# Part of an fp32 matmul in float32r passes, and one subtraction on GpSimd: linear attention and two feed-forward layers

## The chip, the cores and the metric

The kernel runs on one core of one Trainium2 chip. The metric is the device time of one execution in microseconds (us): 1692.37 us is the median of three runs of the kernel before (1692.07 to 1695.33).

## The reference

The program computes a linear attention and two feed-forward layers behind it, in float32:

```python
kv  = np.einsum('bhsd,bhse->bhde', k, v)          # 8 batches, 8 heads, 576 tokens, 64 columns
out = np.einsum('bhsd,bhde->bhse', q, kv)
x   = out / np.sqrt(np.mean(out * out, -1, keepdims=True) + 1e-06) * g_norm   # 4608 tokens x 512
h   = x @ w_in                                     # layer 1: 512 -> 2048 -> 512
g   = (a0 + a1*h + a2*h**2 + a3*h**3) / (1 + |b0|*|h| + |b1|*h**2 + 1e-06)
x   = g @ w_out
h   = x @ moe2_w_in                                # layer 2: the same sizes
g   = np.where(h >= 1, h, np.where(h <= -1, 0, (h + 1)**2 / 4))
y   = g @ moe2_w_out
```

## The kernel before, in words

The 4608 tokens are cut into 9 blocks of 512 (`j` = 0 to 8; the text counts them as block 1 to block 9). A batch has 576 tokens, so a block of 512 mostly lies across two batches: its `q` columns fall into two pieces, 64 + 448, 128 + 384, 192 + 320, 256 + 256 and so on; only the first and the last block lie in one batch.

Phase 0 is the attention and layer 1, phase 1 is layer 2. In phase 0 the attention of block `j + 1` is done in pieces between the layer steps of block `j`. A layer step `f` (16 of them for each block) makes a hidden tile `h` of 128 x 512 with 12 matmuls (lines 441 to 443), its nonlinearity on ScalarE and VectorE (lines 450 to 478), and 12 matmuls into four accumulators (lines 493 to 495). The second half of a step comes `LAG` = 3 steps after the first half, so that there is time for the nonlinearity.

A product in float32 is had in one of two ways. A native fp32 matmul passes over its columns four times; the trace shows it as two MATMUL instructions. The other way splits each operand into a high part (float32r) and a low part (the value less the high part, also float32r), and adds three products: high by high, high by low, low by high. Both layers go the second way. The high part is made by ScalarE (line 184), the low part by a subtraction on VectorE (`subtract`, line 189). In phase 0 the hidden value's parts are `gh` (ScalarE) and `gl` (line 478, VectorE).

The attention of a block has four pairs of heads, `p` = 0 to 3 (function `attention`). For each: `q` is loaded into an `io` buffer, `out_mm` (line 380) multiplies it by the block-diagonal `kvbd` of its batch in native fp32, one matmul for each batch piece; ScalarE squares the result (`sq`), splits it into `sqh` and, on VectorE, `sql` (line 404, names `a<-a,a` fp32r in the trace), and TensorE sums over the head with a matrix of ones (`ms_mm`, lines 390 and 391; only the second of these reads `sql`). The rest scales the output and splits it into `xh` and `xl`. The scratch tiles `a1` to `a4` have one buffer each.

`k^T v` of all batches is made in block 1 and written to DRAM; `kv_fetch` brings it back into one of two `kvbd` buffers. The `raw` ring has four buffers of 4 KB in each partition: batches of k and v and then weights, as they come from DRAM, stand in it until they are decoded.

The order of the instructions is not written out by hand. Every operation is recorded with an engine, a cost and a key (`prog.op`), and `prog.order` plays them through a list scheduler: each engine takes the ready operation with the smallest key. Each engine then works through its own list strictly in order. GpSimd (POOL) has no operation in the kernel before. All DMAs go through SyncE's queue.

Of the kernel before, what the change touches and what calls it, by code (L numbers as in the profile page):

```python
# [121 lines left out]
def kernel(  # L122
# [60 lines left out]
    def activate(key, out, in_, func=AF.Copy, reads=(), cost=C_SB, **kw):  # L183
        op(ACT, cost, key, lambda: nc.scalar.activation(  # L184
            out=out(), in_=in_(), func=func, **{k: v() if callable(v) else v for k, v in kw.items()}
        ), [in_, *reads], [out])

    def subtract(key, out, x, hi):
        op(DVE, C_TT, key, lambda: nc.vector.tensor_tensor(  # L189
            out=out(), in0=x(), in1=hi().bitcast(F32), op=ALU.subtract  # L190
        ), [x, hi], [out])

# [44 lines left out]
    def load(key, t, src, cost=0.7, reads=(), rows=P):  # L237
        op(SP, cost, key, lambda: nc.sync.dma_start(out=t()[:rows], in_=src), reads, [t])
# [120 lines left out]
    def kv_fetch(bb, key):  # L359
# [6 lines left out]

        op(SP, 1.0, key, fetch, [kvs[bb]], [kvbd[bb % 2]])

    def attention(j, p, key, o_ring="o", m_ring="m", tags=("a1", "a2", "a3", "a4")):

        q = new("io", key - 2)
        load(key - 2, q, qT[p][:, j * T:(j + 1) * T])
        o = new(o_ring, key)

        def out_mm():
            t0 = 0
            while t0 < T:
                bb, r = divmod(j * T + t0, S)
                n = min(T - t0, S - r)
                nc.tensor.matmul(  # L380
                    out=o()[:, t0:t0 + n], lhsT=kvbd[bb % 2]()[:, p, :], rhs=q()[:, t0:t0 + n],
                    start=True, stop=True,
                )
                t0 += n

        def ms_mm():
            if native:
                nc.tensor.matmul(out=ms(), lhsT=ones().bitcast(F32), rhs=sq(), start=True, stop=True)
                return
            nc.tensor.matmul(out=ms(), lhsT=ones(), rhs=sqh(), start=True, stop=False)  # L390
            nc.tensor.matmul(out=ms(), lhsT=ones(), rhs=sql(), start=False, stop=True)

        batches = {j * T // S, (j * T + T - 1) // S}
        op(PE, 0.86, key, out_mm, [q, *(kvbd[bb % 2] for bb in batches)], [o])
        native = j < 2
        if native:
            sq, rs, og, e = (new(t, key) for t in tags)
            activate(key, sq, o, AF.Square, cost=C_PS)
        else:
            sq, sqh, sql = new(tags[0], key), new(tags[1], key, F32R), new(tags[2], key, F32R)  # L400
            og, rs, e = new(tags[0], key + 0.1), new(tags[2], key + 0.1), new(tags[3], key)
            activate(key, sq, o, AF.Square, cost=C_PS)
            activate(key, sqh, sq)
            subtract(key, sql, sq, sqh)
        activate(key, og, o, scale=ghalf, cost=C_PS + C_AP)
        ms = new(m_ring, key)
        op(PE, 0.86 if native else 0.43, key, ms_mm, [ones, sq] if native else [ones, sqh, sql], [ms])

        activate(key, rs, ms, AF.Abs_reciprocal_sqrt, cost=C_PS, bias=EPS)
        activate(key, e, rs, AF.Square)  # L410
        add_multiply(key, e, ms, EPS, e)
        add_multiply(key, e, e, -3.0, rs)
        multiply(key, e, og, e)
        xh, xl = new("xh", key, F32R), new("xl", key, F32R)
        activate(key, xh, e)
        subtract(key, xl, e, xh)
        xs[0, j, p] = (xh, xl)

# [14 lines left out]
    def ffn_step(ph, j, f, s):  # L433
        h = new("h", s)
        whi, wlo = wsb[ph, f, 0]
        for p in range(KT):
            xh, xl = xs[ph, j, p]

            def in_mm(p=p, xh=xh, xl=xl):
                c = slice(p * P, (p + 1) * P)  # L440
                nc.tensor.matmul(out=h(), lhsT=whi()[:, c], rhs=xh(), start=(p == 0), stop=False)  # L441
                nc.tensor.matmul(out=h(), lhsT=whi()[:, c], rhs=xl(), start=False, stop=False)  # L442
                nc.tensor.matmul(out=h(), lhsT=wlo()[:, c], rhs=xh(), start=False, stop=(p == KT - 1))  # L443

            op(PE, 0.68, s, in_mm, [whi, wlo, xh, xl], [h])
        k = s + 0.5
        native = ph == 0 and j == 0
        if ph == 0:

            ah, u, t, r = new("ah", k), new("u", k), new("t", k), new("r", k)  # L450
            activate(k, ah, h, AF.Abs, cost=C_PS)
            activate(k, u, ah, AF.Identity, scale=lambda: absb()[:, 1:2], bias=lambda: absb()[:, 0:1], cost=0.71)
            activate(k, t, h, AF.Identity, scale=lambda: na()[:, 3:4], bias=lambda: na()[:, 2:3], cost=0.665)
            multiply(k, u, u, ah)
            multiply(k, t, t, h)
            add_multiply(k, t, t, lambda: na()[:, 1:2], h)
            activate(k, r, u, AF.Abs_reciprocal_sqrt, bias=1.0 + EPS)
            activate(k, r, r, AF.Square)
            add_multiply(k, u, u, 1.0 + EPS, r)
            add_multiply(k, r, t, lambda: na()[:, 0:1], r)  # L460
            if native:
                gh = new("gh", k)
                add_multiply(k, gh, u, -2.0, r)
            else:
                add_multiply(k, u, u, -2.0, r)
                g = u
        else:

            cl, g = new("u", k), new("t", k)
            op(DVE, C_TT, k, lambda: nc.vector.tensor_scalar(  # L470
                out=cl(), in0=h(), scalar1=-1.0, scalar2=1.0, op0=ALU.max, op1=ALU.min
            ), [h], [cl])
            activate(k, cl, cl, AF.Square, scale=0.5, bias=0.5)
            op(DVE, C_TT, k, lambda: nc.vector.tensor_tensor(out=g(), in0=cl(), in1=h(), op=ALU.max), [cl, h], [g])  # L474
        if not native:
            gh, gl = new("gh", k, F32R), new("gl", k, F32R)
            activate(k, gh, g)
            subtract(k, gl, g, gh)

        k = s + LAG + 0.5  # L480
        if f == 0:
            acc[ph, j] = [new(f"acc{m}", k) for m in range(4)]
        wohi, wolo = (w32[f], None) if native else wsb[ph, f, 1]
        first, last = f == 0, f == NF - 1
        for m in range(4):
            o = acc[ph, j][m]

            def out_mm(m=m, o=o):
                c = slice(m * P, (m + 1) * P)
                if native:  # L490
                    nc.tensor.matmul(out=o(), lhsT=wohi().bitcast(F32)[:, c], rhs=gh(), start=first, stop=last)  # L491
                elif ph == 0:
                    nc.tensor.matmul(out=o(), lhsT=wohi()[:, c], rhs=gh(), start=first, stop=False)  # L493
                    nc.tensor.matmul(out=o(), lhsT=wolo()[:, c], rhs=gh(), start=False, stop=False)  # L494
                    nc.tensor.matmul(out=o(), lhsT=wohi()[:, c], rhs=gl(), start=False, stop=last)  # L495
                else:
                    nc.tensor.matmul(out=o(), lhsT=gh()[:, c], rhs=wohi(), start=first, stop=False)  # L497
                    nc.tensor.matmul(out=o(), lhsT=gh()[:, c], rhs=wolo(), start=False, stop=False)  # L498
                    nc.tensor.matmul(out=o(), lhsT=gl()[:, c], rhs=wohi(), start=False, stop=last)  # L499

            op(PE, 0.86 if native else 0.68, k, out_mm, [wohi, gh] if native else [wohi, wolo, gh, gl], [o])
            if last:
                t = new(("r", "r", "a1", "a2")[m] if ph else "io", k)
                activate(k, t, o, cost=C_PS)
                dst = x2d[j, m] if ph == 0 else out[j * T + m * P:j * T + (m + 1) * P, :]
                stored = prog.buf(None)
                op(SP, 0.7, k, lambda t=t, dst=dst: nc.sync.dma_start(out=dst, in_=t()), [t], [stored])
                if ph == 0:
                    x2s[j, m] = stored
# [20 lines left out]
        kv_batch(bb, 1.05 + 2.0 * (bb - 2), 0.45)  # L530
    for j in range(NB):
        s0 = j * NF
        if 2 <= j + 1 < B:
            kv_fetch(j + 1, s0 - 1)
        if j + 1 < NB:
            for p in range(KT):
                attention(j + 1, p, s0 + (0.9 + 3.6 * p if j == 0 else 2.5 + 3.8 * p))
        for f in range(NF):
            ffn_step(0, j, f, s0 + f)
            if j == 0:  # L540
                weight_low(0, f, 1, NF + f + 0.5, w32[f], wsb[0, f, 1][0])
# [57 lines left out]
```

## Time and profile before

| | us |
|---|---|
| median of three runs | 1692.37 |
| the profiled execution, whole | 1694.58 |
| its span, first to last instruction | 1692.8 |

The first page of the profile gives for each engine its busy time, the share of the span and the number of instructions. PE is TensorE's matmuls, PEld its weight loads (which lie beside matmuls), DVE is VectorE, ACT is ScalarE, POOL is GpSimd.

Three views follow below. The windows view gives for a stretch `A:B` (us from the start of the span) its length, then each engine's busy time with its instruction count in brackets, in the order PE, PEld, DVE, ACT, POOL, then the granted TensorE clock (1.00 is 2.4 GHz), the share of the DMA engines and GB/s. The lines view gives line, engine, operation, `out<-in` by the program's names, shapes, count, then busy us and mean ns of one, then idle us of the engine ahead of them and what ended most of it. The timeline gives start in us, duration in us, engine, line, operation and count; a bracket is the idle time just before it and its releaser. A matmul's modelled duration overlaps the next one, and so does a VectorE operation's by some 0.09 us: the pace is read from start to start. Rows with x2 or x4 are neighbours of one line merged into one row; the shape is that of the first.

### The profile page before, as it was taken

The numbers are of one execution on the slowest core, as the hardware profiler recorded it, in microseconds if no ns is written. First come the engines' busy times: TensorE is split into PE (matmuls) and PEld (weight loads), VectorE is DVE, ScalarE is ACT, GpSimd is POOL, SyncE is SP. The second block draws the span as 40 slices with busy tenths as digits, with TensorE's granted clock in tenths as the row PEclk, the third lists the DMA queues.
The fourth block names the chain that finished last, engine by engine and source line by source line (L and its number), as shares of the span: only waits on it lengthen the run. The fifth ranks groups of instructions, "written<-read, shape, count | busy, mean of one in ns | idle before, by whom it ended". The sixth has DMA issues, their size and how long they took to land.

```text
span 1692.8 us, 20528 instructions
## 1 busy us (share of the span) xinstructions
PE 1668.5 (99%) x7688; PEld 1343.0 (79%) x7688; DVE 1197.2 (71%) x1896; ACT 956.5 (57%) x1599; POOL 0.2 (0%) x4
## 2 busy tenths in 40 slices
PE   6999999999999999999999999999999999999999
PEld 4555788888888888888888888888888888888887
DVE  6999999989899998989999963434343434343333
ACT  6777878787877878787886542323232323232222
POOL 0000000000000000000000000000000000000000
PEclk9999999999999999999999999999999999999999
DMA  7667101010100101010214410101010101000000
GB/s 267 221 241 237 58 29 50 4 44 7 47 7 15 39 4 50 1 50 1 75 38 160 162 51 0 51 0 51 0 51 1 50 1 44 7 13 20 0 26 25
DMA packets 40531, 93.07 MB, mean 55 GB/s; under 512 B 7856, under 2 KB 8624, under 8 KB 40432
## 3 DMA queue, kind: packets, MB, share of 16 engines
q1 hardware_dynamic: 40432, 91.77, 16.1%
q8 instruction: 60, 0.98, 0.2%
q14 instruction: 39, 0.32, 0.1%
HBM read 72.09 MB, written 19.66 MB: 54 GB/s over the span
## 4 chain that ended last, share of the span: by engine, by line
PE 93%; DMA 3%; DVE 2%; ACT 1%; issue 0%; SPq 0%; DVEq 0%; ACTq 0%
PE h L441 15%; PE h L443 15%; PE h L442 15%; PE acc L499 8%; PE acc L497 8%; PE acc L498 8%; PE acc L493 7%; PE acc L495 7%; PE acc L494 7%; PE o L380 2%; PE acc L491 1%; DMA raw<-in_w_dram 1%; DMA raw<-in_kv_dram 1%; PE m L321 1%; ACT a L184 0%
## 5 line engine op out<-in xcount | busy, mean ns | idle before, releaser
L441 PE MATMUL h<-xh,wih 128*128 128x512 f32 x1152 | 459.2, 399 | 3.5 <-DVE t L198 2.6
L443 PE MATMUL h<-xh,wil 128*128 128x512 f32 x1152 | 449.3, 390 | 0.0
L442 PE MATMUL h<-xl,wih 128*128 128x512 f32 x1152 | 449.0, 390 | 0.0
L184 ACT ACTIVATE u<-u 128x512 f32<-128x512 f32 x144 | 90.9, 632 | 357.9 <-DVE u L470 357.9
L441 PEld LDWEIGHTS h<-xh,wih 128*128 128x128 f32 x1152 | 216.8, 188 | 54.5 <-DVE t L198 3.8
L442 PEld LDWEIGHTS h<-xl,wih 128*128 128x128 f32 x1152 | 216.7, 188 | 47.7 <-issue 3.3
L443 PEld LDWEIGHTS h<-xh,wil 128*128 128x128 f32 x1152 | 216.7, 188 | 46.2 <-DVE wil L290 0.5
L470 DVE TENSOR_SCALAR u<-h 128x512 f32<-128x512 f32 x144 | 99.6, 691 | 183.7 <-PE h L443 183.7
L497 PE MATMUL acc<-woh,gh 128*128 128x512 f32 x576 | 224.1, 389 | 0.0
L498 PE MATMUL acc<-wol,gh 128*128 128x512 f32 x576 | 224.1, 389 | 0.0
L499 PE MATMUL acc<-woh,gl 128*128 128x512 f32 x576 | 224.1, 389 | 0.0
L198 DVE SCALAR_TENSOR_TENSOR u<-u,r 128x512 f32<-128x512 f32 x272 | 188.2, 692 | 22.9 <-ACT r L184 19.9
L493 PE MATMUL acc<-gh,woh 128*128 128x512 f32 x512 | 202.3, 395 | 0.0
L495 PE MATMUL acc<-gl,woh 128*128 128x512 f32 x512 | 199.4, 389 | 0.0
L494 PE MATMUL acc<-gh,wol 128*128 128x512 f32 x512 | 199.2, 389 | 0.0
L189 DVE TENSOR_TENSOR gl<-t,gh 128x512 fp32r<-128x512 f32 x144 | 99.6, 692 | 130.7 <-ACT gh L184 130.7
L474 DVE TENSOR_TENSOR t<-u,h 128x512 f32<-128x512 f32 x144 | 99.0, 688 | 100.3 <-ACT u L184 100.3
L184 ACT ACTIVATE gh<-t 128x512 fp32r<-128x512 f32 x144 | 90.9, 631 | 132.3 <-PE acc L498 131.7
L498 PEld LDWEIGHTS acc<-wol,gh 128*128 128x128 f32 x576 | 108.2, 188 | 22.6
L499 PEld LDWEIGHTS acc<-woh,gl 128*128 128x128 f32 x576 | 108.1, 188 | 22.4
L497 PEld LDWEIGHTS acc<-woh,gh 128*128 128x128 f32 x576 | 108.0, 188 | 22.3
L184 ACT ACTIVATE r<-u 128x512 f32<-128x512 f32 x144 | 91.1, 633 | 46.7 <-DVE u L194 46.2
(90 smaller groups left out, 2123.4 us busy)
## 6 DMA issues: line engine op xcount, KB each, us to landing
raw<-in_w_dram SPq DMA_DIRECT2D x64, 512.0 KB, 3.9
raw<-in_kv_dram SPq DMA_DIRECT2D x28, 512.0 KB, 4.9
io<-in_qT_dram SPq DMA_DIRECT2D x36, 256.0 KB, 2.9
x2d<-io SPq DMA_DIRECT2D x36, 256.0 KB, 2.3
io<-x2d SPq DMA_DIRECT2D x36, 256.0 KB, 2.7
out_dram<-r SPq DMA_DIRECT2D x18, 256.0 KB, 2.0
out_dram<-a SPq DMA_DIRECT2D x18, 256.0 KB, 3.9
raw<-in_kv_dram SPq DMA_DIRECT2D x7, 256.0 KB, 3.6
```

Source lines behind the costliest of these rows:

```text
L184: op(ACT, cost, key, lambda: nc.scalar.activation(out=out(), in_=in_(), func=func, **{k: v() if callable(v) else v for k, v in kw.items()} ...
L189: op(DVE, C_TT, key, lambda: nc.vector.tensor_tensor(out=out(), in0=x(), in1=hi().bitcast(F32), op=ALU.subtract), [x, hi], [out])
L198: op(DVE, C_STT if callable(add) else C_TT, key, lambda: nc.vector.scalar_tensor_tensor(out=out(), in0=x(), scalar=add() if callable(add) ...
L441: nc.tensor.matmul(out=h(), lhsT=whi()[:, c], rhs=xh(), start=(p == 0), stop=False)
L442: nc.tensor.matmul(out=h(), lhsT=whi()[:, c], rhs=xl(), start=False, stop=False)
L443: nc.tensor.matmul(out=h(), lhsT=wlo()[:, c], rhs=xh(), start=False, stop=(p == KT - 1))
L493: nc.tensor.matmul(out=o(), lhsT=wohi()[:, c], rhs=gh(), start=first, stop=False)
L494: nc.tensor.matmul(out=o(), lhsT=wolo()[:, c], rhs=gh(), start=False, stop=False)
L495: nc.tensor.matmul(out=o(), lhsT=wohi()[:, c], rhs=gl(), start=False, stop=last)
L497: nc.tensor.matmul(out=o(), lhsT=gh()[:, c], rhs=wohi(), start=first, stop=False)
L498: nc.tensor.matmul(out=o(), lhsT=gh()[:, c], rhs=wolo(), start=False, stop=False)
L499: nc.tensor.matmul(out=o(), lhsT=gl()[:, c], rhs=wohi(), start=False, stop=last)
```

## The change

Three parts.

1. From block 3 on (`j >= 2`), a piece of `q` with at least 256 columns is multiplied by `k^T v` in three float32r matmuls where there was one native fp32 matmul. Pieces with fewer columns stay native, as do blocks 1 and 2. For this `q` is split: `qh` on ScalarE into the tile `a2`, `ql` on VectorE into the tile `a4`.
2. `kv_split` splits `kvbd` of batches 1 to 7 into a high and a low half; both stand in one buffer of the `raw` ring until the last block that uses the batch.
3. In blocks 2 to 8 (`1 <= j < NB - 1`) the subtraction for `gl` is done by GpSimd; in block 9 and in phase 1 it stays on VectorE.

The core of the diff:

```diff
-    def subtract(key, out, x, hi):
-        op(DVE, C_TT, key, lambda: nc.vector.tensor_tensor(
+    def subtract(key, out, x, hi, pool=False):
+        op(POOL if pool else DVE, 1.3 if pool else C_TT, key, lambda: (nc.gpsimd if pool else nc.vector).tensor_tensor(
             out=out(), in0=x(), in1=hi().bitcast(F32), op=ALU.subtract
...
+    def kv_split(bb, key):
+        hl = new("raw", key, F32R, (P, 2 * DM))
+        f32 = kvbd[bb % 2]
...
+        op(ACT, C_SB, key, lambda: nc.scalar.activation(out=hl()[:, :DM], in_=src(), func=AF.Copy), [f32], [hl])
+        op(DVE, C_TT, key, lambda: nc.vector.tensor_tensor(
+            out=hl()[:, DM:], in0=src(), in1=hl()[:, :DM].bitcast(F32), op=ALU.subtract
+        ), [f32], [hl])
+        kvr[bb] = hl
...
+        native = j < 2
+        if not native:
+            qh, ql = new(tags[1], key - 0.1, F32R), new(tags[3], key - 0.1, F32R)
+            activate(key - 0.1, qh, q)
+            subtract(key - 0.1, ql, q, qh)
...
+                if not native and n >= T // 2:
+                    w = [kvr[bb]()[:, i * DM + p * P:i * DM + (p + 1) * P] for i in range(2)]
+                    for i, (a, x) in enumerate(((w[0], qh), (w[0], ql), (w[1], qh))):
+                        nc.tensor.matmul(
+                            out=o()[:, t0:t0 + n], lhsT=a, rhs=x()[:, t0:t0 + n], start=(i == 0), stop=(i == 2),
+                        )
+                    t0 += n
+                    continue
...
-            subtract(k, gl, g, gh)
+
+            subtract(k, gl, g, gh, ph == 0 and 1 <= j < NB - 1)
...
+        if j == 1:
+            kv_split(1, s0 - 1)
         if 2 <= j + 1 < B:
             kv_fetch(j + 1, s0 - 1)
+            kv_split(j + 1, s0 - 0.5)
```

The three places in the engines' lists that the prediction speaks of follow. The first is TensorE's list in block 4, where the attention of block 5 (256 + 256 columns) puts its first product into accumulator `o`; `acc` and `h` are the layer's matmuls around it. Before:

```order
L493 MATMUL acc_583_2603<-gh_3277,woh_1597 128x512
L494 MATMUL acc_583_2603<-gh_3277,wol_2045 128x512
L495 MATMUL acc_583_2603<-gl_3288,woh_1597 128x512
L380 MATMUL o_3367<-io_2743,kvbd_75 128x256
L380 MATMUL o_3367<-io_2743,kvbd_74 128x256
L441 MATMUL h_3373<-xh_2656,wih_209 128x512
L442 MATMUL h_3373<-xl_2666,wih_209 128x512
```

And of the change, at the same place:

```order
L526 MATMUL acc_602_2620<-gh_3319,woh_1587 128x512
L527 MATMUL acc_602_2620<-gh_3319,wol_1911 128x512
L528 MATMUL acc_602_2620<-gl_3327,woh_1587 128x512
L405 MATMUL o_3409<-a_714_3238,raw_2374 128x256
L405 MATMUL o_3409<-a_715_3287,raw_2374 128x256
L405 MATMUL o_3409<-a_714_3238,raw_2374 128x256
L405 MATMUL o_3409<-a_714_3238,raw_3231 128x256
L405 MATMUL o_3409<-a_715_3287,raw_3231 128x256
L405 MATMUL o_3409<-a_714_3238,raw_3231 128x256
L473 MATMUL h_3419<-xh_2675,wih_209 128x512
```

The two native matmuls (each is two instructions in the trace) have become two groups of three, whose operands are the tiles `a2`, `a4` and two `raw` buffers; the place between the layer's matmuls is the same.

The second is VectorE's list at the same place: one layer step, with the subtraction for `sql` (`a<-a,a`) in it. Before:

```order
L198 SCALAR_TENSOR_TENSOR t_3345<-t_3345,na,h_3317 128x512
L194 TENSOR_TENSOR u_3364<-u_3364,ah_3343 128x512
L189 TENSOR_TENSOR gl_3377<-u_3307,gh_3370 128x512
L189 TENSOR_TENSOR a_697_3407<-a_695_3381,a_696_3399 128x512
L198 SCALAR_TENSOR_TENSOR u_3364<-u_3364,r_3387 128x512
L198 SCALAR_TENSOR_TENSOR r_3387<-t_3345,na,r_3387 128x512
```

And of the change:

```order
L198 SCALAR_TENSOR_TENSOR t_3387<-t_3387,na,h_3359 128x512
L194 TENSOR_TENSOR u_3406<-u_3406,ah_3385 128x512
L189 TENSOR_TENSOR a_719_3453<-a_717_3427,a_718_3445 128x512
L198 SCALAR_TENSOR_TENSOR u_3406<-u_3406,r_3433 128x512
L198 SCALAR_TENSOR_TENSOR r_3433<-t_3387,na,r_3433 128x512
L198 SCALAR_TENSOR_TENSOR u_3406<-u_3406,r_3433 128x512
```

The row for `gl` is gone from VectorE and stands on GpSimd's list, which holds nothing else in these blocks; the others keep their order.

The third is SyncE's list at the turn from block 1 to block 2: `raw<-in_w_dram` are layer 2's weights, `x2d` the output of layer 1, `io<-in_qT_dram` the `q` of the next attention.

```order
-L238 DMA raw_1518<-in_w_dram 128x512
-L238 DMA raw_1560<-in_w_dram 128x512
-L238 DMA raw_1571<-in_w_dram 128x512
-L238 DMA raw_1595<-in_w_dram 128x512
-L507 DMA x2d<-io_1667 128x512
-L507 DMA x2d<-io_1675 128x512
-L507 DMA x2d<-io_1695 128x512
-L507 DMA x2d<-io_1701 128x512
-L238 DMA io_1718<-in_qT_dram 128x512
-L238 DMA io_1739<-in_qT_dram 128x512
```

The first weights of layer 2 were loaded here, six pieces ahead of their use; now the `raw` buffers hold the split `k^T v`, and these loads stand in blocks 6 to 8 and at the start of block 9, one or two at a time.

## Rows read from the trace of the kernel before

**Rows 1.** First page: busy us, share of the span, instructions.

```profile
PE 1668.5 (99%) x7688; PEld 1343.0 (79%) x7688; DVE 1197.2 (71%) x1896; ACT 956.5 (57%) x1599; POOL 0.2 (0%) x4
```

**Rows 2.** Windows view: two of the blocks the change touches, then block 9.

```profile
363.86:456.36 92.50, 92.50 (x409) 76.61 (x408) 84.68 (x133) 73.98 (x125) 0.00 (x0) 1.00 0.08 25
456.36:548.87 92.51, 92.51 (x410) 76.39 (x408) 84.69 (x133) 74.00 (x125) 0.00 (x0) 1.00 0.08 25
...
826.00:920.00 94.00, 94.00 (x416) 77.86 (x415) 93.79 (x158) 72.72 (x123) 0.00 (x0) 1.00 0.28 93
```

**Rows 3.** Timeline of TensorE: a plain stretch, then native products of q.

```profile
268.63 0.39 PE L493 MATMUL acc<-gh,woh 128*128 128x512 f32 x1
...
270.67 0.39 PE L493 MATMUL acc<-gh,woh 128*128 128x512 f32 x1
...
363.63 0.39 PE L495 MATMUL acc<-gl,woh 128*128 128x512 f32 x1
363.86 1.02 PE L380 MATMUL o<-io,kvbd 128*128 128x256 f32 x4
...
364.95 0.40 PE L442 MATMUL h<-xl,wih 128*128 128x512 f32 x1
...
641.07 0.39 PE L495 MATMUL acc<-gl,woh 128*128 128x512 f32 x1
641.29 1.08 PE L380 MATMUL o<-io,kvbd 128*128 128x448 f32 x4
...
642.50 0.39 PE L442 MATMUL h<-xl,wih 128*128 128x512 f32 x1
...
734.00 0.39 PE L495 MATMUL acc<-gl,woh 128*128 128x512 f32 x1
734.23 1.02 PE L380 MATMUL o<-io,kvbd 128*128 128x512 f32 x2
...
735.32 0.40 PE L442 MATMUL h<-xl,wih 128*128 128x512 f32 x1
```

**Rows 4.** Lines view, whole span: weight loads of line 380.

```profile
L380 PEld LDWEIGHTS o<-io,kvbd 128*128 128x128 f32 x120 | 21.1, 189 | 7.1 <-issue 2.9
```

**Rows 5.** Lines view, 456.4 to 548.9 us: subtractions on VectorE.

```profile
L189 DVE TENSOR_TENSOR gl<-u,gh 128x512 fp32r<-128x512 f32 x16 | 11.0, 688 | 0.8 <-ACT gh L184 0.6
...
L189 DVE TENSOR_TENSOR a<-a,a 128x512 fp32r<-128x512 f32 x4 | 2.8, 688 | 2.0 <-ACT a L184 2.0
```

**Rows 6.** Timeline of VectorE, then of ScalarE: around one `gl`.

```profile
260.57 0.69 DVE L194 TENSOR_TENSOR u<-u,ah 128x512 f32<-128x512 f32 x1
261.18 0.74 DVE L198 SCALAR_TENSOR_TENSOR t<-t,na,h 128x512 f32<-128x512 f32 x1
261.83 0.69 DVE L189 TENSOR_TENSOR gl<-u,gh 128x512 fp32r<-128x512 f32 x1
262.63 0.69 DVE L198 SCALAR_TENSOR_TENSOR u<-u,r 128x512 f32<-128x512 f32 x1
...
260.75 0.63 ACT L184 ACTIVATE gh<-u 128x512 fp32r<-128x512 f32 x1 [0.83 <-DVE u L198]
261.29 0.63 ACT L184 ACTIVATE r<-u 128x512 f32<-128x512 f32 x1
261.96 0.64 ACT L184 ACTIVATE r<-r 128x512 f32<-128x512 f32 x1
...
264.54 0.81 ACT L184 ACTIVATE u<-ah,absb 128x512 f32<-128x512 f32 x1
```

**Rows 7.** Timeline: `sql` on VectorE and the matmul that reads it, twice.

```profile
367.56 0.69 DVE L189 TENSOR_TENSOR a<-a,a 128x512 fp32r<-128x512 f32 x1 [1.96 <-ACT a L184]
...
369.07 0.39 PE L391 MATMUL m<-a,ones 128*128 128x512 f32 x1
...
387.73 0.69 DVE L189 TENSOR_TENSOR a<-a,a 128x512 fp32r<-128x512 f32 x1
...
388.80 0.39 PE L391 MATMUL m<-a,ones 128*128 128x512 f32 x1
```

More of the change, by code (lines that the diff above doesn't have):

```diff
@@ L367, in kv_fetch, with src @@
         op(SP, 1.0, key, fetch, [kvs[bb]], [kvbd[bb % 2]])
+    kvr = {}
+    def kv_split(bb, key):
+        hl = new("raw", key, F32R, (P, 2 * DM))
+        f32 = kvbd[bb % 2]
+        def src():
+            return f32().rearrange("p n d -> p (n d)")
+        op(ACT, C_SB, key, lambda: nc.scalar.activation(out=hl()[:, :DM], in_=src(), func=AF.Copy), [f32], [hl])
[3 more added lines that the diff above has]
+        kvr[bb] = hl
     def attention(j, p, key, o_ring="o", m_ring="m", tags=("a1", "a2", "a3", "a4")):
@@ L393, in attention @@
         batches = {j * T // S, (j * T + T - 1) // S}
-        op(PE, 0.86, key, out_mm, [q, *(kvbd[bb % 2] for bb in batches)], [o])
-        native = j < 2
+        if native:
+            op(PE, 0.86, key, out_mm, [q, *(kvbd[bb % 2] for bb in batches)], [o])
+        else:
+            op(PE, 0.73, key, out_mm, [q, qh, ql, *(t for bb in batches for t in (kvbd[bb % 2], kvr[bb]))], [o])
         if native:
```

## The prediction

> **What bounds the kernel now.** I read the first page for the engine that is busy throughout, then the windows view block by block, then TensorE's timeline at the places that change, and last VectorE and ScalarE around one `gl`. The page shows TensorE busy for 99% of the span and VectorE for 71% [rows 1]; the average hides that VectorE has nearly all its work in phase 0. The windows show it: from one attention product to the next block's, 92.5 us, TensorE is busy for the whole length, the clock is 1.00 (2.4 GHz), and VectorE is busy for 84.7 us, 92% [rows 2]. So in these seven blocks TensorE waits for nothing, and its own work is the bound. A matmul taken away there is worth its pace, and nothing else can make these blocks shorter. VectorE has 7.8 us of idle time in a block to take new work. The two things to price are therefore what TensorE saves, and whether VectorE and GpSimd still deliver in time.
>
> **What TensorE saves.** A plain float32r matmul of 512 columns goes every 0.2267 us (nine from 268.63 to 270.67) [rows 3]. At the granted 2.4 GHz 512 columns are 0.2133 us, so 0.0133 us belongs to the instruction. The native product of q of 512 columns costs this: from the last matmul ahead of it (734.00) to the second behind it (735.32) are 1.32 us, of which 0.453 are two plain paces, so 0.867 us [rows 3], four passes of 0.2133 and one 0.0133. With 256 + 256 columns it is again 0.867 (363.63 to 364.95), with 64 + 448 it is 0.977 (641.07 to 642.50). For pieces of N columns I set three passes of N / 2400 + 0.0133 us, and for a narrow piece that stays native four passes of N / 2400 (and 0.007, half of the 0.0133). For one pair of heads that makes
>
> - block 3 (128 native, 384 wide): 0.220 + 0.520 = 0.74, saves 0.127; block 7 has the same pieces
> - block 4 (192, 320): 0.327 + 0.440 = 0.767, saves 0.10; block 6 the same
> - block 5 (256 + 256, both wide): 6 x 0.120 = 0.72, saves 0.147
> - block 8 (64, 448): 0.217 (from the 0.977 less 0.76 for 448 columns) + 0.60 = 0.817, saves 0.16
> - block 9 (512): 0.68, saves 0.187
>
> Together 0.948 us, times four pairs of heads 3.8 us. That is all that can be had. The bounds: if the 0.0133 us fell away with short passes, 96 x 0.0133 = 1.3 us more (5.1); if a pass could not be shorter than the 0.189 us which a weight load takes [rows 4], 384, 320 and 256 columns would each cost three times 0.189 and only 0.7 us would be left. The row of block 8 speaks against the second: the two instructions for 64 columns, each with its own weight load, cost 0.217 us in all, 0.108 each [rows 3], so loads follow each other faster than their 0.189. I take 3.8.
>
> **What is added, and what hides it.** ScalarE gets one `qh` for each of 28 attentions and seven copies in `kv_split`: five instructions of 0.63 us in a block (the duration of `gh` [rows 6]), 3.2 us beside 74.0 of 92.5 [rows 2]. It stays below 85% and costs nothing. VectorE gets four `ql` and one low half of `k^T v` in a block and loses 16 `gl`, all the same kind of operation of 0.69 us [rows 5], which follow each other at 0.6 (260.57 to 261.18 [rows 6]): 84.7 - 9.6 + 3.0 = 78.1 us, so its idle time grows from 7.8 to 13.8 us in a block of about 92, 0.86 in each of 16 steps. That is the cover for `ql`. In TensorE's list the product that reads `ql` stands about a layer step behind it, so that wait is covered as well.
>
> The w2 loads that moved late cost nothing either: the decoded weights need slots which are free only once block 9 has used the first layer's, and there VectorE is already busy for 93.8 of 94.0 us [rows 2] without TensorE standing. The change moves no `gl` there.
>
> **The subtraction on GpSimd.** The trace has no such operation: POOL is busy for 0.2 us in all [rows 1]. The nearest row is the same subtraction on VectorE, 0.69 us, as the lower end. From above, what counts is how long it may take. In one step `gh` ends at 261.38, and ScalarE writes the next but one `u`, into the buffer that `gl` reads, at 264.54 [rows 6]: 3.1 us in which the subtraction is free for the ring. I take twice VectorE's row, 1.4 us. GpSimd then works a quarter of each step.
>
> The other question is what VectorE does meanwhile. Behind `gh` ScalarE makes the two `r` operations, and VectorE's `u<-u,r` needs the second: it ends at 262.60 and `u<-u,r` starts at 262.63, 1.25 us behind the end of `gh` [rows 6]. VectorE filled just this gap with `t<-t,na,h` (one operand in PSUM) and with `gl` itself. So GpSimd's `gl` falls into a time in which VectorE, without `gl`, has to wait for ScalarE anyway; of 1.4 us 0.15 reaches beyond the gap, against 0.86 of idle time in a step. The Trainium skill (SBUF — State Buffer, Who interferes with whom) says that a VectorE instruction with two SBUF inputs and a GpSimd instruction which reads SBUF exclude each other, the second waiting for the whole of the first. By that rule alone every such pair that meets would be serial; in the gap there is none to meet, and no row here shows GpSimd at work. Its page GPSIMD Engine Reference (section 3.1, Elementwise) gives 4497 ns for 2048 elements, from which I estimate some 1.1 us for 512; with it the subtraction would just fit the gap, and the sum would be the same.
>
> Where the cover is thin is `sql`. The matmul that reads it starts 0.82 us behind the end of `sql` in one attention and 0.38 in the next [rows 7], and there are 28. A delay of VectorE beyond that stops TensorE's whole list. If a GpSimd subtraction stood ahead of all of them for its 1.4 us, they would wait 0.6 and 1.0, 28 x 0.8 = 22 us; with none it is 0. As GpSimd runs a quarter of the time and mostly in ScalarE's gap, I take 0.2 us in all, near the lower end.
>
> **The sum.** -3.8 + 0.2 = -3.6 us, in the profiled execution from 1694.6 (span 1692.8 and 1.8 around it) to 1691.0. That execution was 2.2 us above the median; the saving holds for both, so the median goes from 1692.4 to 1688.8.
>
> **Rivals.**
>
> - *TensorE waits at `sql`.* If VectorE comes later than the list assumes, by the odd GpSimd operation or by `ql` in front, the saving is eaten bit by bit: 0.12 us at each of 28 places is 3.4 us, 1692.1. For it: the 0.38 us, and a saving so small that little is needed. Against it: the idle time of VectorE nearly doubles.
> - *VectorE becomes the bound.* The place is `u<-u,r` behind GpSimd's subtraction: if that holds VectorE for more than its 0.86 us of idle time in each of 112 steps, every step grows by the rest. At 1.0 us this is 112 x 0.14 = 16 us, 1704; it decides (slower by more than 3.4 us) from 0.92 us. For it: operations with two SBUF inputs are more than half of VectorE's, and the attention's stand in no fixed place to `gh`. Against it: the 1.25 us gap. This is the time by the skill's rule if the two engines mostly meet.
> - *Short passes bound by weight loads*, worked out above: 0.7 us saved, 1691.7. The 64-column row is against it.
>
> **How the numbers follow.** What a measurement of this kernel can tell from no change is about 0.2%, 3.4 us, so faster means below 1689.0: the forecast lies just beyond it. I give the forecast 0.45 (0.40 of it below 1689.0), the waits at `sql` 0.27 (0.25 of it within 3.4 us, the rest slower), the weight loads 0.06, VectorE as the bound 0.22. So faster 0.40, same 0.05 + 0.25 + 0.06 = 0.36, slower 0.24. The likeliest case alone spans 1687.3 (the 5.1 us) to 1689.5. The range goes up into the two rivals, to 1699: 10 us of waits for `sql` or the beginning of the VectorE bound.
>
> **What would show it.** Right: the seven stretches in which the attentions of blocks 3 to 9 are done each shorter by 0.4 to 0.75 us in the windows view, TensorE busy throughout; `gl` on POOL of 1 to 1.5 us, ended before `u<-u,r` starts; VectorE at about 85% in these blocks, its operations at 0.69 us. Wrong: waits of TensorE for the `sql` subtraction or for `ql` that add up to microseconds; VectorE's two-input operations longer than 0.69 us beside POOL, or blocks that grow together with VectorE's busy time; three float32r passes of 256 columns above 0.36 us. A `gl` of over 3 us would make ScalarE's `u` wait for POOL.

## The result, and the profile after

The changed kernel takes 1715.46 us (median of four runs, 1714.10 to 1717.54) beside 1692.54 for the kernel before (now four runs): a ratio of 1.0137, 95% interval 1.0125 to 1.0149. It is slower by 23 us where 3.6 us less were forecast. The profiled execution took 1714.46 us with a span of 1712.7, 19.9 us more than the span before.

The windows view of the changed kernel, for the stretch that answers to the second of [rows 2] and for the next; the columns are the same:

```profile
463.51:558.49 94.98, 93.44 (x414) 76.41 (x413) 84.49 (x123) 74.93 (x129) 23.55 (x16) 1.00 0.11 35
558.49:654.80 96.31, 93.53 (x414) 76.35 (x412) 85.77 (x125) 76.22 (x131) 23.60 (x16) 1.00 0.11 35
```

The stretch is 2.5 to 3.8 us longer than the 92.5 us of before, and TensorE is no longer busy throughout. VectorE's busy time has not fallen: 84.5 us, where 78.1 were worked out, although 16 subtractions have left it. GpSimd's list is busy for 23.6 us.

Who TensorE waited for between 170 and 860 us, in the waits view (us in total, times, longest):

```profile
PE m L421 <- DVE a L189: 10.7, 20, 2.0
PE m L420 <- ACT a L184: 4.6, 9, 1.2
```

Both are the sum over the head (lines 390 and 391 of before): L420 reads `sqh`, L421 reads `sql`. Nothing else stops TensorE there. The view counts idle time against modelled ends, so it shows too little. So the waits are counted from start to start: from the matmul ahead of a sum to the one behind its two matmuls there should be three plain paces of 0.2267 us. What is beyond that adds up to 24.5 us over the 28 sums; in the kernel before it is 0.0. All waits at the sums that follow are counted in this way.

The saving on TensorE came as worked out. The product of q of 512 columns, the answer to the last three of [rows 3]:

```profile
751.09 0.39 PE L528 MATMUL acc<-gl,woh 128*128 128x512 f32 x1
751.32 0.84 PE L405 MATMUL o<-a,raw 128*128 128x512 f32 x3
...
752.23 0.39 PE L474 MATMUL h<-xl,wih 128*128 128x512 f32 x1
```

From 751.09 to 752.23 are 1.14 us, less two paces 0.687; the forecast was 0.68, and 0.867 before. The other pieces cost 0.757 (128 + 384), 0.767 (192 + 320), 0.72 (256 + 256) and 0.837 (64 + 448), each within 0.02 us of the forecast. Over all 28 products this comes to 3.7 us less than before. So -3.7 on the products and +24.5 at the sums make 20.8, near the 19.9 us of the span.

The lines view of VectorE between 175 and 845 us, and of GpSimd's `gl`, shows what became of the operations beside GpSimd:

```profile
L198 DVE SCALAR_TENSOR_TENSOR t<-t,na,h 128x512 f32<-128x512 f32 x112 | 82.8, 740 | 0.5
L194 DVE TENSOR_TENSOR t<-t,h 128x512 f32<-128x512 f32 x112 | 76.1, 680 | 3.8 <-ACT t L184 3.5
...
L194 DVE TENSOR_TENSOR u<-u,ah 128x512 f32<-128x512 f32 x112 | 89.6, 800 | 1.1 <-ACT u L184 0.7
L198 DVE SCALAR_TENSOR_TENSOR a<-a,a 128x512 f32<-128x512 f32 x28 | 26.2, 937 | 0.0
L189 DVE TENSOR_TENSOR a<-io,a 128x512 fp32r<-128x512 f32 x27 | 24.8, 917 | 0.2
...
L189 POOL TENSOR_TENSOR gl<-u,gh 128x512 fp32r<-128x512 f32 x112 | 157.4, 1405 | 680.9 <-ACT gh L184 622.2 <-PE h L475 27.8 <-DVE t L198 27.5
```

The two operations with one input in PSUM (`t<-t,h` and `t<-t,na,h`) kept their 0.68 and 0.74 us. Those with two inputs in SBUF are longer: `u<-u,ah` 0.80, `a<-a,a` 0.94 and `ql` (`a<-io,a`) 0.92 us, against 0.69. These means hide two kinds. A held `u<-u,ah` and a held `ql` are in the timeline of VectorE, then of GpSimd, at two places of block 5:

```profile
464.32 0.75 DVE L198 SCALAR_TENSOR_TENSOR t<-t,na,h 128x512 f32<-128x512 f32 x1
464.98 1.78 DVE L194 TENSOR_TENSOR u<-u,ah 128x512 f32<-128x512 f32 x1
...
479.74 1.52 DVE L189 TENSOR_TENSOR a<-io,a 128x512 fp32r<-128x512 f32 x1
...
464.92 1.29 POOL L189 TENSOR_TENSOR gl<-u,gh 128x512 fp32r<-128x512 f32 x1 [3.65 <-ACT gh L184]
...
479.42 1.29 POOL L189 TENSOR_TENSOR gl<-u,gh 128x512 fp32r<-128x512 f32 x1 [5.08 <-ACT gh L184]
```

At 464.92 GpSimd starts its subtraction, which ends at 466.21; `u<-u,ah` starts 0.06 us behind it and ends at 466.76, that is 0.55 us behind GpSimd's end: it stood still until GpSimd was done. This text calls that a hold. `ql` at 479.74 ends 0.55 us behind GpSimd's end (480.71) too. In this trace 62 VectorE operations are longer than 0.8 us, in all by 47 us more than 0.69 each. All 62 started while a GpSimd subtraction ran, and all read two operands in SBUF; 29 operations with an input in PSUM started there too, and none took more than 0.75 us. The other way round holds as well: 35 of GpSimd's 112 subtractions start while VectorE runs an operation with two SBUF inputs and take 1.65 us on average, the other 77 take 1.29. This is the rule of the Trainium skill (SBUF — State Buffer, Who interferes with whom), and the trace agrees: the second waits for the whole of the first.

How the hold reaches TensorE is in the timeline behind the first of these, of ScalarE, then of VectorE and TensorE:

```profile
465.14 0.62 ACT L184 ACTIVATE a<-o 128x512 f32<-128x512 f32 x1
466.80 0.63 ACT L184 ACTIVATE r<-u 128x512 f32<-128x512 f32 x1 [1.03 <-DVE u L194]
467.33 0.58 ACT L184 ACTIVATE io<-acc 128x512 f32<-128x512 f32 x1
467.81 0.62 ACT L184 ACTIVATE a<-a 128x512 fp32r<-128x512 f32 x1
...
468.46 0.69 DVE L189 TENSOR_TENSOR a<-a,a 128x512 fp32r<-128x512 f32 x1 [1.70 <-ACT a L184]
...
468.13 0.39 PE L528 MATMUL acc<-gl,woh 128*128 128x512 f32 x1
468.49 0.50 PE L420 MATMUL m<-a,ones 128*128 128x512 f32 x1
469.21 0.50 PE L421 MATMUL m<-a,ones 128*128 128x512 f32 x1 [0.22 <-DVE a L189]
```

`r` waits 1.03 us for the held `u<-u,ah`; `sqh` (`a<-a` fp32r at 467.81) has its input since 465.76, but stands two places behind `r` in ScalarE's list. `sql` starts at 468.46, behind it. TensorE, which runs its own list in order, reaches the sum before either is done: from start to start its last three matmuls here are 0.36 and 0.72 us apart, where the pace is 0.23.

### The profile page after: what moved, and what is told of

Its sections match the earlier page's. It is cut to its first block, busy times and chain, and to the rows that moved or that the text cites. A ratio compares the mean times of both kernels' runs of the same rounds, so it can differ in the third digit from the quotient of the medians.

```text
span 1712.7 us, 20776 instructions
## 1 busy us (share of the span) xinstructions
PE 1674.6 (98%) x7720; PEld 1344.8 (79%) x7720; DVE 1196.6 (70%) x1819; ACT 968.1 (57%) x1634; POOL 157.6 (9%) x116
## 4 chain that ended last, share of the span: by engine, by line
PE 65%; DVE 20%; ACT 8%; issue 3%; DMA 3%; POOL 0%; SPq 0%; ACTq 0%; DVEq 0%; POOLq 0%
PE h L473 11%; PE h L475 10%; PE h L474 10%; PE acc L532 8%; PE acc L531 8%; PE acc L530 8%; DVE u L198 5%; ACT r L184 3%; PE acc L526 3%; PE acc L527 3%; PE acc L528 3%; DVE r L198 3%; DVE u L194 2%; DVE t L194 2%; DVE a L198 2%
## 5 line engine op out<-in xcount | busy, mean ns | idle before, releaser
L198 DVE SCALAR_TENSOR_TENSOR u<-u,r 128x512 f32<-128x512 f32 x272 | 198.6, 730 | 53.1 <-ACT r L184 51.7
L189 POOL TENSOR_TENSOR gl<-u,gh 128x512 fp32r<-128x512 f32 x112 | 157.4, 1405 | 680.9 <-ACT gh L184 622.2
L184 ACT ACTIVATE gh<-u 128x512 fp32r<-128x512 f32 x128 | 81.0, 633 | 87.0 <-DVE u L198 82.7
```

Source lines behind the costliest of these rows:

```text
L184: op(ACT, cost, key, lambda: nc.scalar.activation(out=out(), in_=in_(), func=func, **{k: v() if callable(v) else v for k, v in kw.items()} ...
L189: op(POOL if pool else DVE, 1.3 if pool else C_TT, key, lambda: (nc.gpsimd if pool else nc.vector).tensor_tensor(out=out(), in0=x(), in1=h ...
L198: op(DVE, C_STT if callable(add) else C_TT, key, lambda: nc.vector.scalar_tensor_tensor(out=out(), in0=x(), scalar=add() if callable(add) ...
```

## The experiments

Two theories stand against each other first. Theory L: GpSimd's hold on VectorE (the lock, in the expectations) makes the sums late. Theory O: the new lists and the added ql, qh and splits do, whoever does `gl`. All ratios are to the kernel before, run on the same chip.

**gl back on VectorE**

```diff
-            subtract(k, gl, g, gh, ph == 0 and 1 <= j < NB - 1)
+            subtract(k, gl, g, gh)
```

> The changed kernel with all gl subtractions left on VectorE; the wide float32r pieces, ql, qh and the split of k^T v stay, and the lists are planned anew. Theory L (the lock): GpSimd's subtraction reads SBUF and holds VectorE's operations with two SBUF inputs, sql comes late, and TensorE waits at the 28 sums over the head; without it the waits at L421 fall from 15.8 us to under 2 and the time is 1688.5 to 1690.5. Theory O (order and load): the added ql, qh and splits leave too little ahead of the sums, whoever does gl; VectorE then has about 3 us more per block than in the kernel before, the waits stay or grow, and the time is above 1705.

Measured: 1688.80 us, ratio 0.9978 (0.9969 to 0.9988); the waits at the sums are 0.1 us. The windows view of this kernel between 175 and 845 us:

```profile
175.00:845.00 670.00, 670.00 (x2995) 556.42 (x2994) 640.54 (x1019) 556.89 (x946) 0.00 (x0) 1.00 0.10 33
```

TensorE is busy throughout, and VectorE is busy for 640.5 of 670 us, 96%, without making it wait. Theory O falls: the added work alone costs nothing. The whole of the 3.7 us is there (0.22% of 1692), and this version is faster than the kernel before by that little, and than the changed kernel by 1.6%.

**The kernel before with gl on GpSimd and nothing else**

```diff
-            subtract(k, gl, g, gh)
+            subtract(k, gl, g, gh, ph == 0 and 1 <= j < NB - 1)
```

in the kernel before, with the changed `subtract`.

> The kernel before with the gl subtraction of blocks 2 to 8 on GpSimd and nothing else changed (native products of q, no splits). Theory L: the same waits at the sums (L391) as in the changed kernel, some 20 to 26 us, and no saving: 1710 to 1719. Theory O: VectorE loses 9.6 us of work in a block and gets none, so nothing waits: 1690 to 1694.

Measured: 1695.85 us, ratio 1.0025 (1.0016 to 1.0034), slower by some 4 us, with 2.5 us of waits, nearly all at the first three sums. Both theories missed their ranges. The hold is there: 34 VectorE operations are longer than 0.8 us, in all by 18 us more than 0.69 each. Yet the waits are a tenth of those in the changed kernel. The lines view of its VectorE, 175 to 845 us, shows where the holds fall:

```profile
L194 DVE TENSOR_TENSOR u<-u,ah 128x512 f32<-128x512 f32 x115 | 78.7, 684 | 1.2 <-ACT u L184 1.2
L189 DVE TENSOR_TENSOR xl<-a,xh 128x512 fp32r<-128x512 f32 x28 | 26.2, 936 | 0.0
```

`u<-u,ah` is not held at all here (0.684 us); `xl` is (0.936), but no sum waits for `xl`. The same place of the timeline as above, in this kernel (VectorE, then GpSimd):

```profile
457.11 0.69 DVE L194 TENSOR_TENSOR u<-u,ah 128x512 f32<-128x512 f32 x1 [0.20 <-ACT u L184]
...
457.73 1.29 POOL L189 TENSOR_TENSOR gl<-u,gh 128x512 fp32r<-128x512 f32 x1 [4.48 <-PE o L380]
```

VectorE starts `u<-u,ah` 0.62 us ahead of GpSimd and is through 0.07 us behind GpSimd's start. In both lists `t<-t,h` and `t<-t,na,h` stand just ahead of it, in this order, and yet in the changed kernel it comes 0.06 us behind GpSimd. The next run shows why.

**The same lists, but GpSimd reads nothing**

```diff
+        if pool:
+            op(POOL, 1.3, key, lambda: nc.gpsimd.memset(out().bitcast(F32), 0.0), [x, hi], [out])
+            return
```

in `subtract`. TensorE, VectorE and ScalarE have the changed kernel's lists, instruction for instruction.

> The changed kernel, with the same lists of TensorE, VectorE and ScalarE instruction for instruction; only GpSimd's subtraction is a memset of gl to zero, which reads no SBUF (the low part of g is left out in blocks 2 to 8). Theory L: VectorE's u<-u,ah goes back to 0.69 us (0.82 in the changed kernel), the waits at the sums fall from 24 us to under 3, and the time is 1688.5 to 1691. Theory O: the lists are what makes TensorE wait, so the time stays at 1712 to 1718.

Measured: 1687.83 us, ratio 0.9974 (0.9965 to 0.9982), 0.4 us of waits at the sums; the time is 0.7 us below the range of Theory L. The windows view and two rows of the lines view, 175 to 845 us:

```profile
175.00:845.00 670.00, 670.00 (x2994) 556.46 (x2993) 582.00 (x905) 554.60 (x944) 58.01 (x110) 1.00 0.11 33
...
L197 DVE TENSOR_TENSOR u<-u,ah 128x512 f32<-128x512 f32 x117 | 80.3, 686 | 5.3 <-ACT u L184 4.6
...
L192 DVE TENSOR_TENSOR a<-io,a 128x512 fp32r<-128x512 f32 x27 | 18.5, 687 | 0.2
```

TensorE is busy throughout, and both operations are back at 0.69 us. The memset is also shorter (0.53 us) and waits for less than the subtraction, but its length is not the reason. In this trace 52 of `u<-u,ah` and `u<-u,r` start while a memset runs, and none takes more than 0.69 us; the 28 that start in its first 0.3 us end 0.2 to 0.4 us behind its end, not 0.55. The memset writes `gl` as the subtraction does and reads nothing. That, and that all held operations are those with two SBUF inputs, speaks for the reads.

As the lists are the same, this trace also shows why `u<-u,ah` came behind GpSimd in the changed kernel. The same place in this run (VectorE, then ScalarE):

```profile
450.92 0.75 DVE L201 SCALAR_TENSOR_TENSOR t<-t,na,h 128x512 f32<-128x512 f32 x1
451.87 0.69 DVE L197 TENSOR_TENSOR u<-u,ah 128x512 f32<-128x512 f32 x1 [0.20 <-ACT u L184]
...
451.71 0.64 ACT L184 ACTIVATE gh<-u 128x512 fp32r<-128x512 f32 x1
```

And in the changed kernel, VectorE 14 us ahead of the place, then ScalarE at it:

```profile
451.02 1.69 DVE L198 SCALAR_TENSOR_TENSOR u<-u,r 128x512 f32<-128x512 f32 x1
...
464.15 0.64 ACT L184 ACTIVATE gh<-u 128x512 fp32r<-128x512 f32 x1
```

Where GpSimd reads nothing, `u<-u,ah` starts 0.48 us ahead of the end of `gh`; in the changed kernel it starts (464.98) 0.19 us behind that end (464.79), and so behind GpSimd. The order is the same, but VectorE is late there from holds before this one: 14 us earlier `u<-u,r`, the next operation behind `ql`, took 1.69 us in place of 0.69. Here one hold brought on the next. Of the twelve held `u<-u,ah` of the changed kernel, six start ahead of the end of `gh` in this run; the other six start behind it here too, so they lie in GpSimd's time by the list alone.

**The sum planned 1.5 us later**

```diff
-                avail[j] = max(avail[j], s + cost + late)
+                avail[j] = max(avail[j], s + cost + late + self.lag[i])
...
-            subtract(key, sql, sq, sqh)
+            subtract(key, sql, sq, sqh, lag=1.5)
```

> The changed kernel, but the scheduler is told that sql arrives 1.5 us later than it thinks, so the sums over the head stand six or seven matmuls further back in TensorE's list; gl stays on GpSimd. If the lock costs only through the thin cover of the sums (VectorE has enough idle time in all), the waits go from 24 us to under 4 and the time is 1689 to 1693. If the lock makes VectorE itself the bound, the wait moves elsewhere and the time stays above 1705.

Measured: 1699.67 us, ratio 1.0047 (1.0035 to 1.0060); the waits at the sums fall from 24.5 to 9.0 us. The expectation was under 4 us of waits and at most 1693. The sums had too little cover, that is, too little time between the end of `sql` and its turn in TensorE's list. But the new order also moves the holds: the waits left are mostly at the third attention of a block, 1.1 to 1.4 us each at six of seven, where all but the first had none before. VectorE did not become the bound.

The two runs that missed asked for a finer theory. Theory G: what counts is which operation stands in GpSimd's time. In the gap behind `gh` (1.25 us in [rows 6]) the lists of the kernel before have operations with two SBUF inputs too (`xl` is one), but hardly one that a sum waits for; the change puts `ql` there, and lets `u<-u,ah` start just behind GpSimd. Theory H: the hold costs the same wherever it falls. Three runs tell them apart.

**Without ql**

```diff
-            qh, ql = new(tags[1], key - 0.1, F32R), new(tags[3], key - 0.1, F32R)
+            qh = ql = new(tags[1], key - 0.1, F32R)
             activate(key - 0.1, qh, q)
-            subtract(key - 0.1, ql, q, qh)
```

> The changed kernel without the 28 subtractions for ql (the second pass reads the high part again, so the low part of q is left out); gl stays on GpSimd. Theory G (the gap is filled): ql, with two SBUF inputs, stands where GpSimd works and is held, and the step behind it brings sql of the second and fourth attention of a block late; without it the waits at these sums (15 of 24.5 us) go, those of the first attention (7 us, from u<-u,ah) may stay: sum of the waits 5 to 12 us, time 1696 to 1703. Theory H (GpSimd's holding alone, wherever it falls): the waits stay near 20 us and the time above 1708.

Measured: 1699.32 us, ratio 1.0038 (1.0025 to 1.0051); waits at the sums 10.3 us, both in the ranges of Theory G. At the fourth attention of a block the waits fall from 7.1 to 0.8 us in all, at the second from 7.9 to 2.8, at the first from 7.1 to 5.1. So `ql` is not all of it at the second.

**u<-u,ah ahead of t<-t,na,h**

```diff
-            add_multiply(k, t, t, lambda: na()[:, 1:2], h)
+            add_multiply(k, t, t, lambda: na()[:, 1:2], h, [u] if 1 <= j < NB - 1 else [])
```

where the last argument is one more operand that only the plan sees: it puts the operation behind `u<-u,ah`.

> The changed kernel with one more edge in the plan for blocks 2 to 8: t<-t,na,h comes behind u<-u,ah on VectorE, so u<-u,ah starts before GpSimd's gl and not 0.06 us behind it. Theory G: u<-u,ah goes back to 0.69 us and the wait of the first attention of a block falls (7 us of 24.5 in all), the others stay: sum of the waits 14 to 20 us, time 1705 to 1711. Theory H: the same hold falls on the next two-input operation and the waits stay at 22 us or more, time above 1712.

Measured: 1703.81 us, ratio 1.0067 (1.0050 to 1.0083); waits at the sums 14.3 us. The lines view, 175 to 845 us:

```profile
L198 DVE SCALAR_TENSOR_TENSOR u<-u,r 128x512 f32<-128x512 f32 x228 | 173.6, 762 | 55.3 <-ACT r L184 52.8
L194 DVE TENSOR_TENSOR u<-u,ah 128x512 f32<-128x512 f32 x114 | 78.0, 684 | 2.1 <-ACT u L184 1.6
...
L189 DVE TENSOR_TENSOR a<-io,a 128x512 fp32r<-128x512 f32 x27 | 18.8, 697 | 0.0
```

`u<-u,ah` is at 0.684 us as expected, and the waits at the first attention of a block fall from 7.1 to 2.2 us. The waits are in the range that Theory G gave, the time is 1.2 us below it; `ql`, too, got out of GpSimd's way (0.697), which may be why. `u<-u,r` now bears more (0.762, from 0.738), and waits of 0.3 to 0.9 us are left at most sums.

**Both**

The two edits above together.

> Both edits: no ql (left out, as in the run without it) and u<-u,ah first. Theory G: no operation with two SBUF inputs that a sum waits for is left in GpSimd's time, as with GpSimd alone in the kernel before; waits under 5 us, time 1689 to 1694. Theory H: waits of 15 us or more, time above 1703.

Measured: 1692.42 us, ratio 1.0002 (0.9993 to 1.0012); waits at the sums 2.7 us, as with GpSimd alone (2.5); both lie in the ranges of Theory G. Two rows of the lines view, 175 to 845 us:

```profile
L189 POOL TENSOR_TENSOR gl<-u,gh 128x512 fp32r<-128x512 f32 x112 | 151.3, 1351 | 664.8 <-ACT gh L184 582.4 <-DVE t L198 43.5 <-PE m L420 14.6
...
L189 DVE TENSOR_TENSOR xl<-a,xh 128x512 fp32r<-128x512 f32 x28 | 26.0, 929 | 0.1
```

Theory G holds: with the operations that a sum waits for out of GpSimd's time, 22 of the 24.5 us are gone, although GpSimd still does all 112 subtractions. Theory H falls: 41 VectorE operations (`xl` above all) are still longer than 0.8 us, by 24 us in all, and the waits are 2.7; in the changed kernel 47 us of holds went with 24.5 us of waits. It is not that TensorE comes to the sums later: 15 or 18 matmuls stand between product and sum in both kernels, but for one sum here with 36. Nor is it the lighter load of VectorE: with `gl` back on VectorE its load is the highest of all runs, and there are no waits. But GpSimd has gained nothing either: this version is level with the kernel before, and the one with `gl` on VectorE is 0.2% faster. Which hold makes which sum late was followed at one place only.

## Why the prediction was wrong

What TensorE saves: right, 3.7 us for 3.8, piece by piece. The weight-load rival falls with the 0.72 us of 256 + 256.

ScalarE's and VectorE's added work cost nothing by itself: right, and with more room than the argument asked for, as VectorE at 96% (gl back on VectorE) shows. That run has the later loads of layer 2's weights too.

The price of the subtraction: 1.29 us undisturbed and 1.40 on average, for 1.4 taken. Right.

The step that failed is "so GpSimd's `gl` falls into a time in which VectorE, without `gl`, has to wait for ScalarE anyway", and with it the term at `sql`, "0.2 us in all, near the lower end". It measured 24.5 us, above even the upper end of 22. The gap was read from one step of the kernel before. In the changed list other operations stand in it: `ql`, which the change itself adds, and `u<-u,ah`, which at the place shown comes 0.06 us behind GpSimd's start because earlier holds have made VectorE late. Even with the lists of the kernel before the gap is not empty, against "in the gap there is none to meet": with GpSimd alone 34 VectorE operations are held. That the waits there are only 2.5 us is owed to which operations these are, and the prediction did not ask who waits for them. Both signs of being wrong that it had named did come: waits for `sql` that add up to microseconds, and operations with two inputs longer than 0.69 us beside POOL. The second flaw is the path: I let a hold reach the sum only through VectorE's own list ("a GpSimd subtraction stood ahead of all of them"), while at 11 of the 28 sums already the first matmul waits, for ScalarE's `sqh`; these make 13.5 of the 24.5 us. At the place shown, ScalarE's `r` waits for the held operation with `sqh` queued behind it.

The slack of 0.38 and 0.82 us [rows 7] was the right place to look, and the rival there was the right mechanism with a price seven times too small: 0.12 us for each sum, where 0.88 was measured. What should have warned me is that both ends had been worked out, 0 and 22, and that the value was put at the low end on the strength of the gap alone.

The rival of VectorE as the bound did not come: it is busy for 84.5 of 95.0 us, the time in holds included, while TensorE waits. "The idle time of VectorE nearly doubles" was also wrong: it went from 7.8 to 10.5 us, not to 13.8, since holds took 6.4 us of what the moved subtractions had left.

Open: how much of the 23 us lies outside the seven stretches. The spans account for 19.9; the medians come from other executions.

## What to carry to other kernels

Before an operation goes to GpSimd, list what VectorE does in the time in which it will run, in the changed order and over many steps, and mark which of these read two SBUF operands and who waits for them: beside GpSimd's 1.3 us each of those was held for up to 1.1 us, while one with an operand in PSUM was not. Count on VectorE being late from one hold when the next comes. A queue with idle time on average hides no hold in front of an in-order consumer that has 0.4 us of cover. And when a change consists of a saving and of a relief meant to make room for it, time the saving alone: here it needed no relief.

## What the runs showed of the hardware

- A GpSimd subtraction of 128 x 512 float32 took 1.29 us undisturbed and 1.65 when it started beside a VectorE operation with two SBUF inputs; such an operation that started during it ended some 0.55 us behind GpSimd's end (up to 1.79 us in place of 0.69), but one with an input in PSUM kept its 0.68 to 0.74 us. Beside a GpSimd memset (0.53 us) operations with two SBUF inputs kept their 0.69 us.
- Three float32r passes keep their price down to 256 columns, 0.12 us a pass, although a weight load of 0.189 us belongs to each.
